# Normalised linear attention and a PReLU feed-forward on one core: batch 2 moves to tokens on partitions, with a refilled opening, a gated load and a spread of g by matmul

## The chip, the core and the metric

The kernel runs on one core of a Trainium2 chip. The metric is device time in microseconds (us). A core has a matrix engine (TensorE, PE in the profile), a vector engine (VectorE, DVE), an activation engine (ScalarE, ACT), a general-purpose engine (GpSimd, POOL) and a queue engine (SyncE, SP). Each takes its instructions in the order in which they were issued to it. Sixteen DMA engines move data between memory (HBM) and on-chip memory (SBUF); matmul results land in PSUM, of which this kernel uses eight buffers of 128 x 512 fp32.

## The reference

Eight batches of eight heads of 576 tokens with head dimension 64 pass a linear attention with an RMS norm per head; the heads are put side by side into 4608 tokens of width 512, which pass two matrix products with a PReLU between them.

```python
kv = np.einsum('bhsd,bhse->bhde', k, v)
out = np.einsum('bhsd,bhde->bhse', q, kv)
rms = np.sqrt(np.mean(out * out, axis=-1, keepdims=True) + 1e-06)
x = out / rms * g_norm            # then heads side by side: (4608, 512)
...
h = x @ w_in                      # 512 -> 2048
g = np.maximum(h, 0.0) + alpha * np.minimum(h, 0.0)
return g @ w_out                  # 2048 -> 512
```

## The kernel before, in words

All engines run in the order in which the program is written (`manual_schedule`), so the place of a call in the code is its place in each engine's queue.

**Tiles.** Tokens are cut into nine windows of 512. For each window w and each of 16 groups g of 128 hidden features, `m1_group` does four matmuls of 128 x 512 into a buffer `h_ps` (three of them, pool `psh`), ACT makes `m_sb` from it, DVE makes `gt` from both and so frees the buffer. `y_mm` then multiplies `gt` with `w_out`, 16 groups for each of four row blocks a, and `y_out` copies the sum on ACT and stores it with two DMAs from SP.

**The order of the feed-forward.** Block 0 runs the first stage of window 0 alone; the y phase (from line 512) runs row blocks 0 to 2 of its second stage; window 1's loop runs its first stage with row block 3 of window 0; from then on window w's first stage runs with window w-1's second stage, and the end is the second stage of the last window.

**Attention, feature form.** For the first `NB_PE` batches (3), features lie on partitions. For each of four pairs j of heads: `step_t` transposes q by five PE matmuls and a DVE copy; `step_kv` makes k'v of the pairs (five matmuls each) and masks it on DVE; `step_ot` makes the attention output and squares it on ACT; `ssq_mm` sums the squares by a matmul with a mask of ones, with ACT's Ln and Exp for the reciprocal root (`rstd`); `norm` multiplies on DVE into `xt`. The rows of these batches that reach past the last whole window are the tail (`step_tail_ot`, `step_tail_ssq`). `window_steps` lists these steps for windows 1 and 2, and the y phase and window 1's loop pop them one by one.

**Attention, token form.** For the other batches a DMA transpose from SP makes `qtm` from the regrouped q (`transpose_q`). A tile of 128 tokens is four matmuls of 128 columns and a square on ACT (`tile_a`), a DVE reduction (`tile_b`), Ln and Exp on ACT and a product `rg` with g on POOL (`tile_c`), and a DVE product `xrow` with DMA transposes from SP into `xm` (`tile_d`). `phase_steps` lays tile i's steps over three groups: a at the end of one, b and c in the next, d at the begin of the one after. c needs g in all partitions, `g_all`, which a DMA from SP brings in window 1.

**Loads.** `load_batch` issues six DMAs on POOL into one of two sets of staging buffers; `regroup` copies k and q into another order, on DVE or on POOL. A load waits in POOL's queue until an earlier one's semaphore is free (eight are in use), and so for DMAs eight places before it.

**Opening.** Batch 0 is loaded in halves of four heads. `keep_warm` runs matmuls whose results nobody reads.

Of the kernel before, what the change touches and what calls it, by code (L numbers as in the profile page):

```python
# [9 lines left out]
FP32 = mybir.dt.float32  # L10
FP16 = mybir.dt.float16
AF = mybir.ActivationFunctionType
ALU = mybir.AluOpType
# [4 lines left out]
def kernel(  # L18
# [11 lines left out]
    nc = tc.nc  # L30

    B, H, S, D = q.shape
# [3 lines left out]
    P = 128  # L36
    NPAIR = H // 2
    W = 512
    NW = N_TOK // W
# [6 lines left out]
    NC = D_MODEL // P  # L46
    assert NC == NPAIR and 0 < REM < P
    inv_d = 1.0 / D
    NB_PE = 3

    const_p = ctx.enter_context(tc.tile_pool(name="constp", bufs=1))
    w_p = ctx.enter_context(tc.tile_pool(name="weights", bufs=1))
# [52 lines left out]
    def regroup(b, nm, h0=0, h1=H, eng=None):  # L105
        (eng or nc.vector).tensor_copy(  # L106
            out=bufs[b % NBUF][nm][:, :, h0:h1, :].rearrange("p t h d -> p h t d"),
            in_=stages[b % NBUF][nm][:, h0:h1],
        )

    def load_batch(b):
        for nm in ("k", "q", "v"):
            load(b, nm)

    def regroup_batch(b):
        for nm in ("k", "q"):
            regroup(b, nm, eng=nc.gpsimd)

    for nm in "qkv":
# [12 lines left out]
    nc.vector.memset(mask32[64:128, 64:128], 1.0)  # L132
    mask16 = const_p.tile([P, P], FP16, name="mask16")
    nc.vector.tensor_copy(out=mask16[:], in_=mask32[:])
    warm16 = const_p.tile([P, W], FP16, name="warm16")
    nc.vector.memset(warm16[:], 0.5)
    eps_t = const_p.tile([P, 1], FP32, name="eps_t")
# [8 lines left out]
    nc.sync.dma_start(out=g2col[64:128, :], in_=g_norm[:].unsqueeze(1))  # L146
    alpha_row = const_p.tile([NF, P], FP32, name="alpha_row")
    nc.sync.dma_start(out=alpha_row[:], in_=moe_alpha[:].rearrange("(g p) -> g p", p=P))
    g_all = const_p.tile([P, D], FP32, name="g_all")


    WQ = 4
# [36 lines left out]
        load_w_out(i)  # L189


    def keep_warm(n):
        ps = ps_s.tile([P, W], FP32, name="warm_ps", tag="s")
        for i in range(n):
            nc.tensor.matmul(out=ps[:], lhsT=mask16[:], rhs=warm16[:], start=True, stop=True)

# [24 lines left out]
    def step_kv(b, j0=0, j1=NPAIR, pool=(ps_s, "s")):  # L221
        if j0 == 0:
            kv_sb = attn_p.tile([P, NPAIR, P], FP16, name="kv_sb")
            for j in range(NPAIR):
                kvs[b, j] = kv_sb[:, j, :]
            kvs[b] = kv_sb
        kv_ps = pool[0].tile([P, j1 - j0, P], FP32, name="kv_ps", tag=pool[1])
        for j in range(j0, j1):
            ks, vs = pair_cols(b, "k", j), pair_cols(b, "v", j)
            for t in range(NT):  # L230
                nc.tensor.matmul(  # L231
                    out=kv_ps[:, j - j0, :], lhsT=ks(t), rhs=vs(t),
                    start=(t == 0), stop=(t == NT - 1),
                )
        nc.vector.tensor_mul(  # L235
            out=kvs[b][:, j0:j1, :], in0=kv_ps[:],
            in1=mask32[:].unsqueeze(1).to_broadcast([P, j1 - j0, P]),
        )
# [8 lines left out]
    def step_ot(w, j, pool=None):  # L247
        if pool is not None:
            ot_ps = pool[0].tile([P, W], FP32, name="ot_ps", tag=pool[1])
        else:  # L250
            ot_ps = ps_o.tile([P, W], FP32, name="ot_ps", tag=f"o{j % 2}")
        n0 = w * W
        while n0 < (w + 1) * W:
            b = n0 // S
            n1 = min((b + 1) * S, (w + 1) * W)
            nc.tensor.matmul(  # L256
                out=ot_ps[:, n0 - w * W : n1 - w * W], lhsT=kvs[b, j],
                rhs=qts[b, j][:, n0 - b * S : n1 - b * S], start=True, stop=True,
            )
            n0 = n1  # L260
        sq = attn_p.tile([P, W], FP16, name="sq_sb")
        nc.scalar.activation(out=sq[:], in_=ot_ps[:], func=AF.Square)  # L262
        ots[w, j] = (ot_ps, sq)

    def step_ssq(w, j):
        ssq_mm(w, j)
        norm(w, j)

    def ssq_mm(w, j):
        ot_ps, sq = ots.pop((w, j))  # L270
        ssq_ps = ps_o.tile([P, W], FP32, name="ssq_ps", tag="o2")
        nc.tensor.matmul(out=ssq_ps[:], lhsT=mask16[:], rhs=sq[:], start=True, stop=True)  # L272
        rstd = attn_p.tile([P, W], FP32, name="rstd")
        nc.scalar.activation(  # L274
            out=rstd[:], in_=ssq_ps[:], func=AF.Ln, bias=eps_t[:], scale=inv_d,
        )
        nc.scalar.activation(out=rstd[:], in_=rstd[:], func=AF.Exp, bias=0.0, scale=-0.5)  # L277
        ots[w, j] = (ot_ps, rstd)

    def norm(w, j):  # L280
        ot_ps, rstd = ots.pop((w, j))
        xts[w, j] = xt_p.tile([P, W], FP16, name="xt", tag=f"xt{j}")
        nc.vector.scalar_tensor_tensor(  # L283
            out=xts[w, j][:], in0=ot_ps[:], scalar=g2col[:], in1=rstd[:],
            op0=ALU.mult, op1=ALU.mult,
        )
# [122 lines left out]
    def window_steps(w):  # L409

        order = "t0 kv t1 o0 t2 s0 o1 t3 s1 o2 - s2 o3 - s3".split()
        fn = {"t": step_t, "o": step_ot, "s": step_ssq}
        one = {"kv": lambda: step_kv(w), "-": lambda: None}
        return [one.get(x) or (lambda x=x: fn[x[0]](w, int(x[1]))) for x in order]
# [4 lines left out]
    def m1_mm(h_ps, w, g, cs):  # L419
        for c in cs:  # L420
            nc.tensor.matmul(  # L421
                out=h_ps[:], lhsT=w_in_blk(c, g), rhs=xt_of(w, c),
                start=(c == 0), stop=(c == NC - 1),
            )
# [11 lines left out]
    def m1_group(w, g):  # L436
        h_ps = ps_h.tile([P, W], FP32, name="h_ps", tag="h")
        m1_mm(h_ps, w, g, range(NC))
        m1_evac(h_ps, w, g)


    def y_mm(y, w, a, g):
        nc.tensor.matmul(  # L443
            out=y[:], lhsT=gts[w, g][:, a * P : (a + 1) * P], rhs=w_out_blk(g),
            start=(g == 0), stop=(g == NF - 1),
        )

    def y_out(y, w, a):
        y_sb = ysb_p.tile([P, D_MODEL], FP32, name="y_sb")
        nc.scalar.copy(out=y_sb[:], in_=y[:])  # L450
        for i in range(0, P, REM):
# [5 lines left out]
                rows = out[b * S + LONG : (b + 1) * S, :].rearrange("(p t) m -> t p m", t=TPP)  # L457
            nc.sync.dma_start(out=rows[t], in_=y_sb[i : i + REM, :])


    H_POOL = (ps_h, "h")
    keep_warm(10)
# [1 line left out]
    step_t(0, 0, H_POOL)  # L464
    step_t(0, 1, H_POOL)
    regroup(0, "k", 0, HH)
    keep_warm(3)
    step_kv(0, 0, 2)
    step_ot(0, 0)
    step_ot(0, 1)  # L470
    regroup(0, "q", HH, H)
# [11 lines left out]
    )  # L483
    regroup(0, "k", HH, H)
    ssq_mm(0, 0)
    ssq_mm(0, 1)
    step_kv(0, 2, 4)
    norm(0, 0)
    norm(0, 1)
    step_ot(0, 2)  # L490
    step_ot(0, 3, (ps_y, "y"))
    load_batch(2)
    first = [ps_h.tile([P, W], FP32, name="h_ps", tag="h") for g in range(3)]
    for g in range(3):
        m1_mm(first[g], 0, g, (0, 1))
    step_ssq(0, 2)
    keep_warm(2)
    step_ssq(0, 3)
    for g in range(3):
        m1_mm(first[g], 0, g, (2,))  # L500
    for g in range(3):
        m1_mm(first[g], 0, g, (3,))
        m1_evac(first[g], 0, g)
    for g in range(3, NF):
        m1_group(0, g)
        if g == 10:
            regroup(1, "k")
        if g == 14:
            regroup(1, "q")

# [9 lines left out]
    for g in range(NF):  # L520
        for a in range(AHEAD):
            y_mm(ys[a], 0, a, g)
            if a != 1 and steps and n - len(steps) < n * (AHEAD * g + a) // (AHEAD * (NF - 3)):
                steps.pop(0)()
    for a in range(AHEAD):
        y_out(ys[a], 0, a)
    regroup_batch(2)


    steps = window_steps(2)  # L530
    n = len(steps)
    y = ps_y.tile([P, W], FP32, name="y_ps", tag="y")
    for g in range(NF):
        if g == 3:
            load_batch(3)
            regroup_batch(3)
        m1_group(1, g)
        if g > 3 and steps:
            steps.pop(0)()
        y_mm(y, 0, AHEAD, g)  # L540
        if g > 3 and steps:
            steps.pop(0)()
        if g == NF - 4:
            nc.sync.dma_start(out=g_all[:], in_=g_norm[:].partition_broadcast(P))
        if g == NF - 3:
            transpose_q(3)
    y_out(y, 0, AHEAD)

    LOAD_G = 6
    for w in range(2, NW):
        steps = phase_steps(w + 1)
        for g in range(NF):
            if g == LOAD_G and w + 2 < B:
                load_batch(w + 2)
            a, part = divmod(g, TPW)
            if part == 0:
                pool, tag = ((ps_y, "y"), (ps_s, "s"))[a % 2]  # L560
                y = pool.tile([P, W], FP32, name="y_ps", tag=tag)
            begin, mid, end = steps.pop(0) if steps else ([], [], [])
            for f in begin:
                f()
            m1_group(w, g)
            for f in mid:
                f()
            for gg in range(part * TPW, (part + 1) * TPW):
                y_mm(y, w - 1, a, gg)
            if part == TPW - 1:  # L570
                y_out(y, w - 1, a)
            for f in end:
                f()
            if g == LOAD_G + 3 and w + 2 < B:
                regroup_batch(w + 2)
            if g == NF - 3 and w + 2 < B:
                transpose_q(w + 2)
# [35 lines left out]
```

## Time and profile before

| | |
|---|---|
| median of 6 runs (lowest to highest) | 304.49 us (303.85 to 305.35) |
| the profiled execution | 305.58 us |
| its span, first to last instruction | 303.8 us |
| mean granted clock | 0.989 |
| PE busy | 283.7 us, 93% of the span |
| DVE, ACT, POOL busy | 163.2, 156.5, 96.6 us |
| first-stage and second-stage matmuls of 128 x 512 | 1,152 |

The groups of instructions that weigh most, from the page (line, engine, operation, output<-inputs, shape and count, then busy us and mean ns of one, then the engine's idle time before them and what ended most of it):

```profile
L430 DVE SCALAR_TENSOR_TENSOR gt<-m_sb,beta_sb,h_ps 128x512 f16<-128x512 f32 x144 | 106.7, 744 | 79.3 <-ACT m_sb L428 78.2
L428 ACT ACTIVATE m_sb<-h_ps 128x512 f32<-128x512 f32 x144 | 85.7, 597 | 89.9 <-PE h_ps L421 89.7
L363 POOL TENSOR_TENSOR rg<-ss,g_all 128x512 f32<-128x512 f32 (+1 forms) x25 | 26.1, 1044 | 92.9 <-ACT ss L361 92.9
```

Matmuls are pipelined: the page gives a 128 x 512 one 379 ns from begin to end, while in a dense stretch one starts every 0.216 us (four in 0.86 us). An engine's busy share is an average over stages that have different limits; idle time of an engine that isn't the last to finish costs nothing.

### The profile page before, as it was taken

The page shows a single profiled execution, that of the slowest core. Times are in us where ns is not written, and L with a number is a line of the kernel's source. Part 1 is how long each engine was busy: PE and PEld are TensorE (multiplying, and loading weights), DVE is VectorE, ACT ScalarE, POOL GpSimd, SP SyncE. Part 2 cuts the span into 40 slices and gives each one's busy share as a digit, 9 for nine tenths or more (in the row PEclk, how much of TensorE's full clock was granted, in tenths as well). Part 3 has the DMA queues.
Part 4 walks back from the last instruction along what each step waited for, and adds up shares of the span by engine and source line. Part 5 has one row for each costly group of instructions (what it writes and reads, how often), then busy time and mean ns, then how long its engine had stood idle before and what let it go on. Part 6 is the DMA issues. An engine that isn't in the chain of part 4 may idle for free.

```text
span 303.8 us, 4204 instructions
## 1 busy us (share of the span) xinstructions
PE 283.7 (93%) x1526; PEld 136.5 (45%) x1526; DVE 163.2 (54%) x249; ACT 156.5 (52%) x298; POOL 96.6 (32%) x105
## 2 busy tenths in 40 slices
PE   5476999988999899999999999999999999999993
PEld 2232454453554355445544544455445444444441
DVE  4526953557665548544864585459546844344200
ACT  1256627749586348444843573458437544443320
POOL 9733315640018604660575055504101300000000
PEclk9969999999999999999999999999999999999999
DMA  7999999894117972995289839954311411112233
GB/s 88 171 206 200 203 204 184 124 216 90 35 35 99 197 181 28 144 224 127 54 118 212 155 68 146 185 122 74 75 35 37 95 35 35 37 39 55 46 70 69
DMA packets 61156, 34.33 MB, mean 113 GB/s; under 512 B 27840, under 2 KB 56528, under 8 KB 61136
## 3 DMA queue, kind: packets, MB, share of 16 engines
q0 software_dynamic: 29664, 18.35, 43.3%
q1 hardware_dynamic: 31472, 15.71, 24.1%
q8 instruction: 12, 0.20, 0.3%
q14 instruction: 8, 0.07, 0.1%
HBM read 36.74 MB, written 9.44 MB: 152 GB/s over the span
## 4 chain that ended last, share of the span: by engine, by line
PE 82%; ACT 5%; POOL 4%; DVE 3%; issue 2%; DMA 2%; POOLq 0%; ACTq 0%; DVEq 0%
PE h_ps L421 37%; PE y_ps L443 35%; PE kv_ps L231 3%; DMA qst<-in_q_dram 2%; PE otm_ps L339 2%; ACT rstd L274 2%; ACT m_sb L428 2%; POOL rg L363 1%; DVE gt L430 1%; PE qt_ps L210 1%; PE ssq_ps L272 1%; PE yc L443 1%; PE yb L443 1%; PE ya L443 1%; ACT rstd L277 1%
## 5 line engine op out<-in xcount | busy, mean ns | idle before, releaser
L430 DVE SCALAR_TENSOR_TENSOR gt<-m_sb,beta_sb,h_ps 128x512 f16<-128x512 f32 x144 | 106.7, 744 | 79.3 <-ACT m_sb L428 78.2
L443 PE MATMUL y_ps<-w_out_sb,gt 128*128 128x512 f16 x528 | 134.8, 379 | 0.0
L428 ACT ACTIVATE m_sb<-h_ps 128x512 f32<-128x512 f32 x144 | 85.7, 597 | 89.9 <-PE h_ps L421 89.7
L421 PE MATMUL h_ps<-xm,w_in_sb 128*128 128x512 f16 x384 | 98.5, 379 | 0.0
L421 PEld LDWEIGHTS <-w_in_sb 128*128 128x128 f16 x576 | 55.5, 98 | 67.4 <-issue 8.2
L443 PEld LDWEIGHTS <-gt 128*128 128x128 f16 x576 | 55.9, 98 | 65.9 <-issue 2.2
L363 POOL TENSOR_TENSOR rg<-ss,g_all 128x512 f32<-128x512 f32 (+1 forms) x25 | 26.1, 1044 | 92.9 <-ACT ss L361 92.9
L421 PE MATMUL h_ps<-xt,w_in_sb 128*128 128x512 f16 x192 | 48.4, 384 | 3.7 <-DVE gt L430 2.2
L450 ACT COPY y_sb<-y_ps 128x512 f32<-128x512 f32 x33 | 19.2, 582 | 17.5 <-PE y_ps L443 17.4
L351 DVE TENSOR_REDUCE ss<-sqm_sb 128x8 f32<-128x512 f32 (+1 forms) x25 | 17.1, 683 | 8.2 <-ACT sqm_sb L345 8.2
L106 POOL COPY ksb<-kst 128x2560 f16<-128x2560 f16 x6 | 13.9, 2318 | 21.6 <-DMA kst<-in_k_dram 21.6
L372 DVE TENSOR_TENSOR xrow<-otm_ps,rg 128x512 f16<-128x512 f32 (+1 forms) x25 | 17.0, 682 | 6.3 <-POOL rg L363 6.3
L345 ACT ACTIVATE sqm_sb<-otm_ps 128x512 f32<-128x512 f32 (+1 forms) x25 | 14.8, 593 | 6.9 <-PE otm_ps L339 6.9
L106 POOL COPY qsb<-qst 128x2560 f16<-128x2560 f16 x6 | 13.9, 2321 | 10.6 <-DMA qst<-in_q_dram 6.1
L283 DVE SCALAR_TENSOR_TENSOR xt<-ot_ps,g2col,rstd 128x512 f16<-128x512 f32 x12 | 8.9, 749 | 13.1 <-ACT rstd L277 13.1
L262 ACT ACTIVATE sq_sb<-ot_ps 128x512 f16<-128x512 f32 x12 | 6.9, 588 | 16.4 <-PE ot_ps L256 16.4
L231 PE MATMUL kv_ps<-vst,ksb 128*128 128x128 f16 x160 | 10.9, 225 | 2.8 <-DMA vst<-in_v_dram 1.4
L231 PEld LDWEIGHTS <-ksb 128*128 128x128 f16 x160 | 10.1, 101 | 6.5 <-issue 3.7
L274 ACT ACTIVATE rstd<-ssq_ps,eps_t 128x512 f32<-128x512 f32 x12 | 8.2, 685 | 6.5 <-PE ssq_ps L272 6.5
L339 PEld LDWEIGHTS <-qtm 128*128 128x128 f16 x100 | 7.7, 98 | 5.9
L339 PE MATMUL otm_ps<-kv_sb,qtm 128*128 128x128 f16 x100 | 9.7, 219 | 0.0
L235 DVE TENSOR_TENSOR kv_sb<-kv_ps,mask 128x512 f16<-128x512 f32 (+1 forms) x9 | 5.6, 627 | 6.3 <-PE kv_ps L231 6.3
(56 smaller groups left out, 134.7 us busy)
## 6 DMA issues: line engine op xcount, KB each, us to landing
out_dram<-y_sb SPq DMA_DIRECT2D x72, 128.0 KB, 2.4
kst<-in_k_dram POOLq DMA_DIRECT2D x7, 320.0 KB, 5.0
qst<-in_q_dram POOLq DMA_DIRECT2D x7, 320.0 KB, 8.5
vst<-in_v_dram POOLq DMA_DIRECT2D x7, 320.0 KB, 10.9
w_in_sb<-in_moe_w_in_dram POOLq DMA_DIRECT2D x4, 512.0 KB, 10.6
w_out_sb<-in_moe_w_out_dram POOLq DMA_DIRECT2D x4, 512.0 KB, 16.2
kst<-in_k_dram POOLq DMA_DIRECT2D x7, 256.0 KB, 6.5
qst<-in_q_dram POOLq DMA_DIRECT2D x7, 256.0 KB, 9.8
```

What stands on the lines that cost most here:

```text
L106: (eng or nc.vector).tensor_copy(out=bufs[b % NBUF][nm][:, :, h0:h1, :].rearrange("p t h d -> p h t d"), in_=stages[b % NBUF][nm][:, h0:h1],)
L231: nc.tensor.matmul(out=kv_ps[:, j - j0, :], lhsT=ks(t), rhs=vs(t), start=(t == 0), stop=(t == NT - 1),)
L339: nc.tensor.matmul(out=ot_ps[:, 2 * j : 2 * j + 2, :], lhsT=qtms[b][:, t * NPAIR + j, :], rhs=kvs[b, j], start=True, stop=True,)
L345: nc.scalar.activation(out=sq[0:n], in_=ot_ps[0:n], func=AF.Square)
L351: nc.vector.tensor_reduce(out=ss[0:n], in_=sq[0:n], op=ALU.add, axis=mybir.AxisListType.X,)
L363: nc.gpsimd.tensor_tensor(out=rg[0:n], in0=ss[0:n].unsqueeze(2).to_broadcast([n, H, D]), in1=g_all[0:n].unsqueeze(1).to_broadcast([n, H, D ...
L372: nc.vector.tensor_mul(out=x[0:n], in0=ot_ps[0:n], in1=rg[0:n])
L421: nc.tensor.matmul(out=h_ps[:], lhsT=w_in_blk(c, g), rhs=xt_of(w, c), start=(c == 0), stop=(c == NC - 1),)
L428: nc.scalar.activation(out=m_sb[:], in_=h_ps[:], func=AF.Relu, scale=-1.0)
L430: nc.vector.scalar_tensor_tensor(out=gt[:], in0=m_sb[:], scalar=beta_sb[:, g : g + 1], in1=h_ps[:], op0=ALU.mult, op1=ALU.add,)
L443: nc.tensor.matmul(out=y[:], lhsT=gts[w, g][:, a * P : (a + 1) * P], rhs=w_out_blk(g), start=(g == 0), stop=(g == NF - 1),)
L450: nc.scalar.copy(out=y_sb[:], in_=y[:])
```

## The change

- `NB_PE` goes from 3 to 2: batch 2 is computed in token form. The loop of window 2's attention steps within window 1 goes, and window 1 uses the general loop with `phase_steps`, keeping one y matmul for each group. The tail is then 128 columns wide and one step for all four pairs.
- The tiles of batch 2 come in windows 1 and 2. Its q is regrouped on DVE and transposed by DMA after group 9 of the y phase; its k is regrouped on DVE after group 13.
- The load of batch 3 stands after group 13 of the y phase. Ahead of it, a POOL copy of one element of batch 2's `qtm` waits for that transpose.
- From batch 2 on q is loaded and regrouped ahead of k.
- `g_all` is made after group 12 of block 0: DVE scales the identity by g, a matmul with ones spreads it over all partitions, DVE copies it out. The DMA for it goes.
- Opening: more `keep_warm` matmuls, before the first `step_ot`, between the sums of squares, and around the first groups; `norm` of pair 0 ahead of `step_kv` of pairs 2 and 3; the sum of squares of pair 2 after one group's first two matmuls, in a PSUM buffer of its own, where it came after three groups' and shared one.

```diff
-    NB_PE = 3
+    NB_PE = 2
...
     def load_batch(b):
-        for nm in ("k", "q", "v"):
+        for nm in ("q", "k", "v"):
             load(b, nm)
...
+    def spread_g():
+
+        diag = const_p.tile([P, D], FP32, name="diag")
+        nc.vector.tensor_scalar(
+            out=diag[0:D], in0=ident[0:D, 0:D], scalar1=g2col[0:D], scalar2=None, op0=ALU.mult,
+        )
+        g_ps = ps_y.tile([P, D], FP32, name="g_ps", tag="y")
+        nc.tensor.matmul(
+            out=g_ps[:], lhsT=ones32[0:D], rhs=diag[0:D], start=True, stop=True,
+        )
+        nc.vector.tensor_copy(out=g_all[:], in_=g_ps[:])
...
-    keep_warm(3)
+    keep_warm(4)
     step_kv(0, 0, 2)
+    keep_warm(2)
     step_ot(0, 0)
...
     ssq_mm(0, 0)
+    keep_warm(3)
     ssq_mm(0, 1)
+    norm(0, 0)
+    keep_warm(3)
     step_kv(0, 2, 4)
-    norm(0, 0)
     norm(0, 1)
-    step_ot(0, 2)
+    step_ot(0, 2, (ps_o, "o2"))
     step_ot(0, 3, (ps_y, "y"))
...
-    for g in range(3):
+    m1_mm(first[0], 0, 0, (0, 1))
+    ssq_mm(0, 2, (ps_s, "s"))
+    for g in (1, 2):
         m1_mm(first[g], 0, g, (0, 1))
-    step_ssq(0, 2)
-    keep_warm(2)
-    step_ssq(0, 3)
+    ssq_mm(0, 3, (ps_o, "o0"))
+    keep_warm(6, (ps_o, "o1"))
+    norm(0, 2)
+    norm(0, 3)
     for g in range(3):
         m1_mm(first[g], 0, g, (2,))
+    keep_warm(2, (ps_o, "o1"))
...
         if g == 10:
             regroup(1, "k")
+        if g == 12:
+            spread_g()
...
+        if g == 9:
+            regroup(2, "q")
+            transpose_q(2)
+        if g == 13:
+
+            gate = const_p.tile([1, 1], FP16, name="gate")
+            nc.gpsimd.tensor_copy(out=gate[:], in_=qtms[2][0:1, 0, 0:1])
+            load_batch(3)
+            regroup(2, "k")
     for a in range(AHEAD):
         y_out(ys[a], 0, a)
-    regroup_batch(2)
...
-    steps = window_steps(2)
-    n = len(steps)
-    y = ps_y.tile([P, W], FP32, name="y_ps", tag="y")
-    for g in range(NF):
-        if g == 3:
-            load_batch(3)
-            regroup_batch(3)
-        m1_group(1, g)
-        if g > 3 and steps:
-            steps.pop(0)()
-        y_mm(y, 0, AHEAD, g)
-        if g > 3 and steps:
-            steps.pop(0)()
-        if g == NF - 4:
-            nc.sync.dma_start(out=g_all[:], in_=g_norm[:].partition_broadcast(P))
-        if g == NF - 3:
-            transpose_q(3)
-    y_out(y, 0, AHEAD)
...
-    for w in range(2, NW):
+    for w in range(1, NW):
         steps = phase_steps(w + 1)
         for g in range(NF):
-            if g == LOAD_G and w + 2 < B:
+            if g == LOAD_G and 3 < w + 2 < B:
                 load_batch(w + 2)
             a, part = divmod(g, TPW)
...
+            parts = range(part * TPW, (part + 1) * TPW)
+            if w == 1:
+                a, parts = AHEAD, [g]
```

## The prediction

> **What bounds the kernel now.** I read the chain of waits first, then busy time by stage, then the granted clock in 2 us stretches, then the timeline around each wait.
>
> ```profile
> PE 82%; ACT 5%; POOL 4%; DVE 3%; issue 2%; DMA 2%; POOLq 0%; ACTq 0%; DVEq 0%
> ```
>
> TensorE (PE) sets the end, so only PE work removed and PE idle time removed count. By stage (columns: us, then PE, weight loads, DVE, ACT, POOL busy, PE clock, DMA share, GB/s):
>
> ```profile
> 0.00:26.72 26.72, 15.64 (x77) 7.08 (x78) 11.42 (x30) 10.04 (x16) 16.87 (x30) 0.87 1.12 162
> 26.72:38.37 11.65, 11.38 (x52) 5.07 (x52) 9.98 (x15) 7.31 (x13) 4.22 (x7) 1.00 1.34 202
> 38.37:54.51 16.14, 15.28 (x102) 7.72 (x101) 6.84 (x12) 8.10 (x14) 6.84 (x6) 1.00 1.19 178
> 54.51:78.92 24.41, 22.09 (x134) 11.04 (x133) 16.32 (x25) 16.82 (x31) 7.82 (x7) 1.00 0.79 134
> 78.92:110.16 31.24, 30.39 (x168) 14.95 (x167) 17.44 (x27) 18.21 (x36) 11.86 (x11) 1.00 0.74 124
> 110.16:139.80 29.64, 29.64 (x166) 14.54 (x164) 17.40 (x26) 15.82 (x32) 12.87 (x12) 1.00 0.82 133
> 139.80:169.66 29.86, 29.86 (x169) 14.74 (x168) 18.54 (x28) 16.83 (x35) 13.91 (x13) 1.00 0.75 128
> ```
>
> The rows are: opening; rest of block 0; y phase of window 0; window 1; windows 2, 3 and 4. From window 3 on PE never idles, and nothing there changes. All that can move is the first 110 us: 11 us idle in the opening, a window 1 of 24.4 us and a window 2 that takes 1.4 us more than window 4.
>
> The clock, in 2 us stretches (same columns):
>
> ```profile
> 12.00:14.00 2.00, 1.00 (x12) 0.83 (x13) 1.08 (x3) 0.71 (x2) 2.00 (x3) 0.96 1.33 176
> 14.00:16.00 2.00, 1.22 (x6) 0.52 (x5) 1.09 (x3) 1.49 (x3) 1.85 (x4) 0.50 1.27 205
> 18.00:20.00 2.00, 1.97 (x5) 0.71 (x5) 0.64 (x1) 1.09 (x2) 0.77 (x1) 0.50 1.24 205
> 20.00:22.00 2.00, 1.84 (x7) 0.69 (x6) 0.00 (x0) 0.55 (x1) 0.69 (x1) 0.84 1.24 206
> 50.00:52.00 2.00, 2.00 (x12) 0.82 (x11) 0.52 (x1) 1.50 (x4) 1.36 (x2) 1.00 1.40 198
> 52.00:54.00 2.00, 1.81 (x9) 0.78 (x8) 0.75 (x1) 1.50 (x4) 2.00 (x2) 1.00 0.47 69
> ```
>
> The clock is halved from about 13.8 to 20.7 us, when a 512-column matmul takes 0.43 instead of 0.216 us. The DMA engines are loaded to 52.8 us without a break: the loads through batch 2, in the order issued, set what can arrive when. The waits concerned, from the timeline (start, length, engine, line, in brackets the idle time before):
>
> ```profile
> 24.87 0.81 PE L421 MATMUL h_ps<-xt,w_in_sb 128*128 128x512 f16 x3 [0.43 <-DVE xt L283]
> ...
> 35.12 0.82 DVE L106 COPY ksb<-kst 128x2560 f16<-128x2560 f16 x1
> 35.85 2.06 DVE L430 SCALAR_TENSOR_TENSOR gt<-m_sb,beta_sb,h_ps 128x512 f16<-128x512 f32 x3
> ...
> 48.39 2.32 POOL L106 COPY ksb<-kst 128x2560 f16<-128x2560 f16 x1 [7.23 <-DMA kst<-in_k_dram]
> ...
> 61.69 1.28 PE L231 MATMUL kv_ps<-vst,ksb 128*128 128x128 f16 x20 [1.34 <-DVE qt_sb L219]
> ...
> 68.78 2.60 SPq L329 DMA_TRANSPOSE qtm<-qsb  x1
> ...
> 98.24 0.69 DVE L372 TENSOR_TENSOR xrow<-otm_ps,rg 128x512 f16<-128x512 f32 x1 [3.71 <-POOL rg L363]
> ...
> 99.64 1.02 PE L421 MATMUL h_ps<-xt,w_in_sb 128*128 128x512 f16 x4 [0.85 <-DVE gt L430]
> ```
>
> **What the Trainium skill says.** "TensorE: Matmul & The Clock Gate", Part 1 (What's actually happening): the array's clock is halved or full, decided over free-running stretches of 3.4 us, and drops after an idle one. The trace agrees on length (13.8 to 20.7 is two of them) but not on "idle": in the 3.4 us before the drop PE was busy 1.7 us, while 2.0 us busy (20.7 to 24.1) kept the clock. The same page (Architectural detail) says VectorE and ScalarE queues are strictly first in, first out; the trace agrees (at 98.24 DVE stands 3.71 us behind one operand, and the evacuations after it stand too). "DMA: Bandwidth & Descriptors", Issuing engines are not separate DMA queues: transfers from SP and POOL share the same 16 engines. Here a transpose of q lands in 4.1 to 5.7 us, those of x in 2.3 to 7.8.
>
> **Part 1, the opening.** Before, the chain to the third stage of block 0 is: kv of pairs 2, 3, ot, six first-stage matmuls at half clock, ssq, two ACT operations (0.69+0.63), the same again, norm (0.75), and the last quarter of the first groups at 24.87. After, fillers cover 11.2-11.6, 14.0-14.7 and 15.2-15.9; ssq of pair 2 comes after two first-stage matmuls, not six, and has its own buffer. At full clock: kv 15.9-16.6, mask on DVE to 17.0 (norm of pair 0 is already done), ot 17.1-17.6, squares to 18.6; w_in's first quarter lands at 18.1 (POOL's queue waits for it then), so two matmuls 18.1-18.5, ssq 18.55-18.9, Ln and Exp of pair 2 to 20.3, of pair 3 to 21.6, norm to 22.4, last quarter at 22.45. Gain 2.4. If the clock stays halved over 13.8-17.2, the fillers take 2.6 us instead of 1.3 and the same sum ends at 23.4: gain 1.5. The 0.43 us filler before ot lifts PE's busy time before 13.8 from 1.7 to 2.1 us, above the 2.0 that kept the clock, so I take 2.4. The filler delays ot by 0.43, which the wait for q's second half (12.4) hides.
>
> **Part 2, g spread in block 0.** The DMA of g (0.65 on SP) goes, which nothing waited for. In its place, after group 12, a DVE operation, an fp32 matmul and a DVE copy. The matmul waits for `diag`, which stands in DVE's queue behind the evacuation of group 12, and PE does nothing else meanwhile. Group 12's matmuls end at 35.36; DVE, 0.8 us late from the copy of k (35.12), evacuates it 36.54-37.22; diag, at the 0.17 of the smallest tensor-scalar here, to 37.4; the matmul 0.2 to 0.5 (alpha's fp32 one takes 0.23), so group 13 starts 2.3 us later. In return two of PE's waits for freed buffers there (0.27 before an h, 0.17 before yc) go. Following DVE on (copy of g, groups 13 and 14, q of batch 1, 0.82), the first transpose of the y phase moves from 39.9 to 41.9: cost 2.0, bounds 1.6 and 2.3. It cannot be free, for no PE work is ordered between.
>
> **Part 3, y phase.** q of batch 2 is now loaded where k was, so it lands at 48.4. Its regroup moves from POOL (2.32) to DVE (0.82), behind the second norm: about 50.5-51.3. SP issues the transpose 51.35-53.95, before the outputs at 54.9, so these aren't delayed; it lands 4.2 later, 55.5. Loads end at 52.8, so the two barely meet. k's regroup stands behind the last norm (55.1): 55.1-55.9, and kv of batch 2 waits for it: 0.5 us of PE, counted in part 4. The gate stands on POOL until 55.5; behind it are six issues of batch 3's load (4.2 us, to 59.8 instead of 57.7) and the first rg (needed at 63). The load ends some 2 us later, near 70; its k regroup ends by 73, before window 2 wants it at 78. Cost 0; 1:1 for PE where that slack is used up.
>
> **Part 4, window 1.** Removed: 20 transposes, 4 ot and 4 ssq (1.1 and 8 x 0.216); added: three tiles of 4 x 0.055 and the tail, 1,024 columns (0.43), which before came in window 2. PE: 80 x 0.216 = 17.3, kv 1.12, tail 0.43, tiles 0.66, kv's wait 0.5, last norm's 0.15: 20.2 against 24.4. But the groups are short here (5 matmuls, 1.08), and each tile brings ACT 0.60+0.30+0.21 and DVE 0.69+0.69. Placed by queue order with these durations, DVE frees h of groups 4, 5 and 6 at 65.85, 67.95 and 69.6, where PE comes at 64.95, 67.0 and 69.05: 2.4 us of waits. Window 1 ends at 77.15, not 78.92: gain 1.8. Bounds: no waits (gain 4.2), or all of the removed work given back (0).
>
> **Part 5, window 2.** Two tail steps and three tiles become five tiles, as in window 4. The tiles start at once, so their rg are through before the next load's six issues at group 6; the 3.71 us DVE wait at 98.24 and PE's 0.85 go. 31.24 becomes window 4's 29.86: gain 1.4; the tail work is in that. I take 1.2, for the first POOL copies may overlap an rg.
>
> Sum: -2.4 + 2.0 + 0 - 1.8 - 1.2 = -3.4. The profiled execution took 305.58 (span 303.8), so 302.2; against the median 304.49, which is 1.09 lower, **301.1**.
>
> **Rivals.**
> - *Window 1 is set by DVE and ACT.* DVE was 67% and ACT 69% busy there already, with shorter groups to come; against: the PE work removed is as sure. Gain of part 4 gone: 302.9.
> - *No waits there.* The buffers hold three groups, and back-to-back evacuations take 0.69, not 0.75. Part 4 gives 4.2: 298.7.
> - *The clock falls behind the spread.* Two us of PE idle in block 0 leave about 1.4 us busy in a 3.4 us stretch that contains them, and 1.7 dropped the clock at 13.8. Against: the wait may straddle two stretches. Price 6.9 us at half speed, 3.45: 304.5.
> - *Slower: the transpose of q of batch 2 is late.* PE reaches the first tile near 60 and stands in order until qtm lands; gate, load and rg stand with it. It has 4.5 us of slack beyond 4.2; PE pays 1:1 past 8.7 us. The x transposes took up to 7.8 instead of 2.5 among loads, three times; three times 4.2 lands at 64.3, costing 4.3: 305.4. It decides against the gain from 63.5 on. Against: loads end before it.
>
> **How the numbers follow.** Forecast 0.48 (its own range 300.2 to 302.2), window 1 bound 0.16, no waits 0.12, clock 0.12, late transpose 0.12. 0.3% (0.9 us) is about what a measurement here can tell from no change. Faster 0.73 (the first three, less 0.03 for costs at their worst), same 0.14, slower 0.13. The range 299.0 to 304.6 leaves out the late transpose and half of the no-waits case.
>
> **What would show it.** Right: clock 1.00 over 14 to 20 us; last quarter of the first groups near 22.5; PE idle about 2 us after group 12, released by DVE diag; window 1 about 22.7 us with waits for gt in groups 7 to 9; window 2 about 29.9 with no wait of xrow for rg beyond 1 us. Wrong: qtm landing after 60, kv of batch 2 waiting for a load, or a clock of 0.5 after 15 us.

## The result, and the profile after

| | before | after |
|---|---|---|
| median (lowest to highest) | 304.58 us (302.48 to 306.76), 35 runs | 302.23 us (301.27 to 303.28), 16 runs |
| profiled execution, span, mean clock | 305.58, 303.8, 0.989 | 302.95, 301.0, 0.994 |

Ratio 0.9925, 95% interval 0.9905 to 0.9946: 2.3 us faster, where 3.4 were forecast. The chain of waits of the kernel after has PE at 85% where it had 82%:

```profile
PE 85%; POOL 3%; ACT 3%; DVE 3%; DMA 3%; issue 2%; POOLq 0%; ACTq 0%
```

Busy time by stage of the kernel after (us, then PE, weight loads, DVE, ACT, POOL busy, PE clock, DMA share, GB/s), in the cuts of the table before: opening, rest of block 0, y phase, windows 1 and 2:

```profile
0.00:23.17 23.17, 16.64 (x92) 7.60 (x93) 11.51 (x31) 9.93 (x16) 16.60 (x29) 1.00 1.11 164
23.17:38.56 15.39, 13.44 (x54) 5.72 (x54) 10.75 (x17) 7.31 (x13) 6.30 (x8) 0.89 1.33 202
38.56:54.41 15.85, 15.16 (x102) 7.72 (x101) 7.28 (x13) 8.10 (x14) 0.68 (x1) 1.00 1.29 184
54.41:77.00 22.59, 19.95 (x118) 9.76 (x117) 16.86 (x25) 14.43 (x30) 11.93 (x12) 1.00 1.14 178
77.00:107.20 30.20, 30.20 (x171) 14.96 (x170) 19.19 (x29) 17.31 (x36) 13.92 (x13) 1.00 0.77 130
```

The opening is 3.55 us shorter and keeps the clock throughout; its end in PE's timeline:

```profile
17.04 0.61 PE L422 MATMUL h_ps<-xt,w_in_sb 128*128 128x512 f16 x2 [0.21 <-DMA w_in_sb<-in_moe_w_in_dram]
...
21.32 0.81 PE L422 MATMUL h_ps<-xt,w_in_sb 128*128 128x512 f16 x3
```

Block 0 then gives 3.74 back, at a clock of 0.89. Windows 1 and 2 bring the rest. The product k'v (kv) of batch 3 starts window 2's work and that of batch 4 window 3's, first in the kernel before, then in the kernel after:

```profile
79.78 1.28 PE L231 MATMUL kv_ps<-vst,ksb 128*128 128x128 f16 x20
...
110.86 1.28 PE L231 MATMUL kv_ps<-vst,ksb 128*128 128x128 f16 x20
```

```profile
78.06 1.28 PE L232 MATMUL kv_ps<-vst,ksb 128*128 128x128 f16 x20
...
107.92 1.28 PE L232 MATMUL kv_ps<-vst,ksb 128*128 128x128 f16 x20
```

The start of window 1 is only 0.10 earlier, so window 1 gained 1.6 us and window 2 gained 1.2.

The timeline of PE in block 0 of the kernel after (start, length, engine, line, in brackets the idle time before):

```profile
23.17 8.79 PE L422 MATMUL h_ps<-xt,w_in_sb 128*128 128x512 f16 x40 [1.03 <-DVE gt L431]
33.91 0.43 PE L470 MATMUL g_ps<-diag,ones 64*128 64x64 f32 x2 [1.95 <-DVE diag L466]
34.28 4.45 PE L422 MATMUL h_ps<-xt,w_in_sb 128*128 128x512 f16 x12
```

and the same kernel in stretches of 2 us (columns as above):

```profile
32.00:34.00 2.00, 0.09 (x1) 0.09 (x1) 1.86 (x4) 0.59 (x1) 0.66 (x2) 1.00 1.35 197
34.00:36.00 2.00, 2.00 (x7) 0.87 (x8) 0.22 (x1) 0.11 (x1) 1.28 (x2) 0.66 1.37 204
36.00:38.00 2.00, 2.00 (x6) 0.76 (x5) 0.75 (x1) 0.89 (x2) 0.75 (x2) 0.50 1.24 206
```

PE stands 1.95 us for `diag`, and behind that the clock is halved for some 3.4 us: the 12 matmuls of groups 13 to 15 take 4.28 us until the y phase instead of 2.6 at 0.216. This is the prediction's clock rival, and it comes on top of the forecast.

PE's waits from there on, in the timeline of the kernel after:

```profile
55.80 1.29 PE L232 MATMUL kv_ps<-vst,ksb 128*128 128x128 f16 x20 [0.36 <-DVE ksb L106]
...
61.11 0.38 PE L340 MATMUL otm_ps<-kv_sb,qtm 128*128 128x128 f16 x4 [1.20 <-DVE xm L314]
...
67.83 1.02 PE L422 MATMUL h_ps<-xt,w_in_sb 128*128 128x512 f16 x4 [0.49 <-DVE gt L431]
69.65 1.02 PE L422 MATMUL h_ps<-xt,w_in_sb 128*128 128x512 f16 x4 [0.58 <-DVE gt L431]
```

The second was in no sum of the forecast: the first tile takes the PSUM buffer o0, which the tail's `xm` still reads (`tag=f"o{i % 2}"`). In window 2 neither PE's wait of 0.85 nor the wait of `xrow` for `rg` of 3.71 is left; the longest of `xrow` is 0.50. The transpose of q and the gate, on SP's and POOL's queues:

```profile
51.18 3.53 SPq L330 DMA_TRANSPOSE qtm<-qsb  x1
...
56.53 0.18 POOL L555 COPY gate<-qtm 1x1 f16<-1x1 f16 x1 [16.54 <-DMA qtm<-qsb]
```

It landed at 56.5, 4.6 us ahead of the first tile and 3.4 ahead of PE's coming to that tile (59.9, where it stands 1.20 us for `xm`).

### The profile page after: what moved, and what is told of

Same layout as the page of the kernel before. It is cut to its first block, busy times and chain, and to the rows that moved or that the text cites. A ratio compares the mean times of both kernels' runs of the same rounds, so it can differ in the third digit from the quotient of the medians.

```text
span 301.0 us, 4238 instructions
## 1 busy us (share of the span) xinstructions
PE 284.4 (94%) x1530; PEld 136.4 (45%) x1530; DVE 166.8 (55%) x255; ACT 153.1 (51%) x298; POOL 98.5 (33%) x109
## 4 chain that ended last, share of the span: by engine, by line
PE 85%; POOL 3%; ACT 3%; DVE 3%; DMA 3%; issue 2%; POOLq 0%; ACTq 0%
PE h_ps L422 39%; PE y_ps L444 37%; PE kv_ps L232 3%; DMA w_in_sb<-in_moe_w_in_dram 3%; PE otm_ps L340 2%; DVE gt L431 1%; ACT m_sb L429 1%; PE yc L444 1%; PE yb L444 1%; PE ya L444 1%; PE warm_ps L196 1%; PE ssq_ps L273 1%; DVE ksb L106 1%; PE qt_ps L211 0%; POOL vst L100 0%
## 5 line engine op out<-in xcount | busy, mean ns | idle before, releaser
L422 PE MATMUL h_ps<-xm,w_in_sb 128*128 128x512 f16 x448 | 115.0, 379 | 0.0
L364 POOL TENSOR_TENSOR rg<-ss,g_all 128x512 f32<-128x512 f32 (+1 forms) x30 | 31.3, 1042 | 86.1 <-ACT ss L362 85.2
L422 PE MATMUL h_ps<-xt,w_in_sb 128*128 128x512 f16 x128 | 32.9, 395 | 2.3 <-DVE gt L431 2.1
L352 DVE TENSOR_REDUCE ss<-sqm_sb 128x8 f32<-128x512 f32 (+1 forms) x30 | 20.5, 683 | 9.6 <-ACT sqm_sb L346 9.6
L346 ACT ACTIVATE sqm_sb<-otm_ps 128x512 f32<-128x512 f32 (+1 forms) x30 | 17.8, 592 | 9.3 <-PE otm_ps L340 9.3
L373 DVE TENSOR_TENSOR xrow<-otm_ps,rg 128x512 f16<-128x512 f32 (+1 forms) x30 | 20.4, 681 | 3.6 <-POOL rg L364 3.6
L196 PE MATMUL warm_ps<-warm,mask 128*128 128x512 f16 x30 | 9.6, 457 | 3.8 <-DVE eps_t L140 3.3
L263 ACT ACTIVATE sq_sb<-ot_ps 128x512 f16<-128x512 f32 x8 | 4.5, 589 | 15.6 <-PE ot_ps L257 15.6
L232 PE MATMUL kv_ps<-vst,ksb 128*128 128x128 f16 x160 | 10.4, 219 | 1.2 <-DMA vst<-in_v_dram 0.8
L284 DVE SCALAR_TENSOR_TENSOR xt<-ot_ps,g2col,rstd 128x512 f16<-128x512 f32 x8 | 6.0, 749 | 9.1 <-ACT rstd L278 9.1
L359 ACT ACTIVATE ss<-ss,eps_t 128x8 f32<-128x8 f32 (+1 forms) x30 | 9.0, 301 | 3.1 <-DVE ss L352 3.1
## 6 DMA issues: line engine op xcount, KB each, us to landing
w_in_sb<-in_moe_w_in_dram POOLq DMA_DIRECT2D x4, 512.0 KB, 10.4
```

Of the source, the lines that this page charges most:

```text
L232: nc.tensor.matmul(out=kv_ps[:, j - j0, :], lhsT=ks(t), rhs=vs(t), start=(t == 0), stop=(t == NT - 1),)
L346: nc.scalar.activation(out=sq[0:n], in_=ot_ps[0:n], func=AF.Square)
L352: nc.vector.tensor_reduce(out=ss[0:n], in_=sq[0:n], op=ALU.add, axis=mybir.AxisListType.X,)
L364: nc.gpsimd.tensor_tensor(out=rg[0:n], in0=ss[0:n].unsqueeze(2).to_broadcast([n, H, D]), in1=g_all[0:n].unsqueeze(1).to_broadcast([n, H, D ...
L373: nc.vector.tensor_mul(out=x[0:n], in0=ot_ps[0:n], in1=rg[0:n])
L422: nc.tensor.matmul(out=h_ps[:], lhsT=w_in_blk(c, g), rhs=xt_of(w, c), start=(c == 0), stop=(c == NC - 1),)
```

## The clock behind the spread of the times

Every execution comes with a mean granted clock. 124 executions of the kernel before, which ran beside the experiments, fall into steps of about 0.005, which is one halved stretch of 3.4 us in 301 (half of 3.4, over 301, is 0.0056). Eight more, of 307.26 us and above, with clocks of 0.975 to 0.981, are left out:

| mean clock | executions of before | median us (lowest to highest) |
|---|---|---|
| 0.996 to 1.0 | 29 | 302.97 (302.56 to 303.65) |
| 0.992 to 0.995 | 44 | 304.33 (303.45 to 305.21) |
| 0.986 to 0.991 | 24 | 305.20 (304.19 to 306.43) |
| 0.980 to 0.985 | 27 | 306.58 (305.04 to 307.13) |

So the time follows the number of halved stretches over most of the spread of 302.5 to 307, and the profiled execution of before, at 0.989, had two. Of the 16 executions of after, ten had 0.996 or more (median 302.00) and six less (302.94): three at 0.993 or 0.994, which fits one halved stretch, and three at 0.990, which fits two. At a kept clock the whole change is worth about 1.0 us; the other 1.3 of the median would then be stretches that the opening no longer loses, less those that the spread of g loses. I give this number for the experiments too, as "at a kept clock": the median of the executions at 0.996 or more, and how many of them. It sorts executions by what came of them; that those which keep the clock differ in nothing else, the arrival of their loads for instance, isn't shown. They are few and from several chips (the kernel before at a kept clock has 302.77 to 303.16 by chip), so differences under 0.4 us between them mean little.

## The experiments

Each was timed against the kernel before on the same chip.

**The opening alone** (the kernel before, with the `keep_warm`, `ssq_mm` and `norm` lines of the change's opening and their buffers, nothing else; the middle of it):

```diff
-    for g in range(3):
+    m1_mm(first[0], 0, 0, (0, 1))
+    ssq_mm(0, 2, (ps_s, "s"))
+    for g in (1, 2):
         m1_mm(first[g], 0, g, (0, 1))
-    step_ssq(0, 2)
-    keep_warm(2)
-    step_ssq(0, 3)
+    ssq_mm(0, 3, (ps_o, "o0"))
+    keep_warm(6, (ps_o, "o1"))
+    norm(0, 2)
+    norm(0, 3)
```

> The kernel before with the changed opening alone (fillers, order of norms and sums, PSUM buffers), nothing else. Theory: clock 1.00 through the opening, last quarter of the first groups near 22.4 instead of 24.9 (2.4 us earlier), and all of it reaches the end: 302.1. Rival (part of the 3.5 us seen in the changed kernel's trace were faster loads of that execution, or the y phase waits for w_out's first quarter, which landed at 35.95): under 1.5 us gained, above 303.

Measured 302.44 us, ratio 0.9926 (0.9903 to 0.9948); at a kept clock 302.43 (21 of 22). It gives as much as the whole change, 2.3 us by the ratio. But where the kernel before keeps its clock too, it is worth only 0.5 us against 302.97 (0.7 against 303.16, the nine on the same chip); the rest of the 2.3 goes with its nearly always keeping it.

**Nine of the opening's fillers alone**, to part clock and order:

```diff
-    keep_warm(3)
+    keep_warm(4)
     step_kv(0, 0, 2)
+    keep_warm(2)
...
     ssq_mm(0, 0)
+    keep_warm(3)
     ssq_mm(0, 1)
+    keep_warm(3)
```

> The kernel before with nothing of the change but nine of the opening's fillers (one more before kv of pairs 0 and 1, two before the first ot, three after each of the sums of squares of pairs 0 and 1); order and buffers of the opening as before. Of 98 executions of the kernel before, the 20 with a mean clock of 0.996 or more have a median of 303.0 us, the 78 with less lie from 303.45 up. Theory (the opening's gain is mostly the clock it keeps, the shorter order of its sums of squares is worth about 0.5 us): nearly all executions have a mean clock of 0.995 or more, median 302.7 to 303.3 us, between the opening of the change alone (302.44) and the kernel before (304.2 to 305.0). Rival 1 (the gain is the order of the sums of squares and their buffers): about 304.5 us, as before. Rival 2 (order and clock both, with the full gain only together): about 303.7 us, the clock dropping once in many executions.

Measured 303.49 us (302.84 to 304.61), ratio 0.9976 (0.9954 to 0.9997). Of 22 executions 18 had 0.996 or more (median 303.38). The fillers mostly keep the clock, where 29 of 124 executions of the kernel before did, but 303.49 lies 0.2 above the theory's band. At a kept clock these fillers cost about 0.4 us themselves (302.97 to 303.38), and the rest of the opening is worth 0.9 (303.38 to 302.43), not 0.5. By the ratios the nine fillers bring 0.7 of the opening's 2.3 us, so that the second rival is right that the gain needs more than them, though not in its clock. The rest is the order, the PSUM buffers and the eight fillers around the first groups (for two before); no run parts these. Its stretches of 2 us (columns as above):

```profile
14.00:16.00 2.00, 1.32 (x13) 0.83 (x12) 0.58 (x2) 1.40 (x3) 1.01 (x2) 1.00 1.24 206
16.00:18.00 2.00, 1.45 (x7) 0.67 (x7) 1.16 (x2) 1.03 (x2) 0.77 (x1) 1.00 1.24 207
20.00:22.00 2.00, 0.81 (x3) 0.29 (x3) 1.43 (x2) 1.26 (x3) 0.19 (x1) 1.00 1.25 207
22.00:24.00 2.00, 0.84 (x4) 0.32 (x4) 0.90 (x3) 1.46 (x3) 0.49 (x1) 1.00 1.26 203
```

PE is busy 1.65 us of the four from 20 to 24 and the clock stays at 1.00, while in the kernel before 1.7 of 3.4 us came ahead of a drop: how much busy time in which stretch keeps the clock isn't settled here.

**g by DMA in the opening instead of the spread**, which was to price the spread:

```diff
+    g_all = const_p.tile([P, D], FP32, name="g_all")
+    nc.sync.dma_start(out=g_all[:], in_=g_norm[:].partition_broadcast(P))
...
-        if g == 12:
-            spread_g()
```

> The changed kernel, but g comes into all partitions by one DMA in the opening; the spread after group 12 of block 0 is gone. Theory (PE's wait for diag costs 2.0 us, and in some executions it also drops the clock for 3.4 us, another 1.7): stretch from group 3 of block 0 to the y phase falls from 15.4 to about 11.7 us, no clock below 1 after 7 us, time 2 to 3.7 us under the changed kernel, so 298.5 to 300.2. Rival (the wait only fills a gap that the loads or DVE's backlog would open anyway): the same time as the changed kernel, 302.2, within 0.5.

Measured 302.90 us, ratio 0.9945 (0.9923 to 0.9966): no gain over the kernel after. PE no longer waits in block 0, but DVE's timeline shows a loss earlier, first here, then in the kernel after:

```profile
9.56 0.49 DVE L106 COPY qsb<-qst 128x1280 f16<-128x1280 f16 x1 [5.13 <-DMA qst<-in_q_dram]
```

```profile
5.59 0.64 DVE L106 COPY qsb<-qst 128x1280 f16<-128x1280 f16 x1 [1.17 <-DMA qst<-in_q_dram]
```

The DMA of g, 32 KB to 128 partitions, was issued at 2.64 and landed 6.6 us later; the first load of q beside it came 4 us late, and in the stretch from 14 to 16 us the clock is 0.50. This execution, of 304.10 us, is one of the slowest of the 22, so the 4 us are not typical; but 13 of the 22 have a mean clock under 0.996, where the opening alone had one of 22. The run prices an early DMA of g, not the spread.

**Batch 2 alone, with g by DMA** (the last kernel with the opening of the kernel before; of its edit):

```diff
-    keep_warm(4)
+    keep_warm(3)
     step_kv(0, 0, 2)
-    keep_warm(2)
...
-    m1_mm(first[0], 0, 0, (0, 1))
-    ssq_mm(0, 2, (ps_s, "s"))
-    for g in (1, 2):
+    for g in range(3):
         m1_mm(first[g], 0, g, (0, 1))
```

> The changed kernel with the opening of before, and g by a DMA in the opening: the move of batch 2 alone. Theory: window 1 falls from 24.4 to 22.8 us and window 2 from 31.2 to 30.0: 3.0 us, 301.5. Rival (the gain of windows 1 and 2 hangs on the earlier opening): under 1 us.

Measured 305.40 us, ratio 1.0025 (0.9995 to 1.0055). The early DMA of g stands in the way again: 11 of its 14 executions had a mean clock of 0.985 or less, where the same kernel with the early spread in place of the DMA, below, has 3 of 22. By which path is not shown: in its trace the first copy of q is at 6.96, hardly later than in the profiled executions without such a DMA (5.57 to 6.73). It doesn't tell what batch 2 is worth.

**The wait for `diag` filled** (eight fillers ahead of the matmul in `spread_g`).

```diff
+        keep_warm(8)
         g_ps = ps_y.tile([P, D], FP32, name="g_ps", tag="y")
```

> The changed kernel with eight unread matmuls (1.7 us) ahead of the spread's matmul. The wait stays, but PE is busy during it. Theory that the clock drop is a cost of its own: clock stays 1.00, y phase 1.5 to 1.7 us earlier than in the changed kernel's profiled execution, median lower by up to 1 us (the drop came in part of the executions only), about 301.3. Rival (the drop doesn't come from the wait, or costs nothing because DVE is behind anyway): no change, 302.2.

Measured 301.78 us, ratio 0.9926 (0.9901 to 0.9952), every one of 6 executions at 0.996 or more. PE's timeline:

```profile
23.52 8.79 PE L422 MATMUL h_ps<-xt,w_in_sb 128*128 128x512 f16 x40 [1.03 <-DVE gt L431]
34.27 0.43 PE L471 MATMUL g_ps<-diag,ones 64*128 64x64 f32 x2 [0.22 <-DVE diag L466]
...
37.23 0.38 PE L444 MATMUL ya<-w_out_sb,gt 128*128 128x512 f16 x1
```

From the first row to the y phase it is 13.71 us. Before it was 11.65: the spread at this place costs 2.06, and the other 1.68 of the kernel after's 3.74 were the clock. What that brings in time isn't shown: the medians differ by 0.45, but the ratios to the kernel before (0.9926 and 0.9925) don't. For the clock there are more executions: in six kernels with the changed opening in which PE doesn't stand idle for `diag` in block 0 and g comes by no DMA (this one, and those from the early spread on that keep the opening and the gate), 49 of 52 have 0.996 or more, in the kernel after ten of 16.

**The spread early**, where the opening waits for its loads anyway (`spread_g()` moved).

```diff
     keep_warm(4)
+    spread_g()
     step_kv(0, 0, 2)
...
-        if g == 12:
-            spread_g()
```

> The changed kernel with the spread of g moved into the opening, behind the first k regroup and ahead of the first kv, where PE waits for v anyway; same three instructions, no DMA. Theory (the wait behind group 12 is the price that eats the opening's gain): no PE wait for diag in block 0, clock 1.00 there, y phase begins near 36.5 instead of 38.6, time 2 us or more under the changed kernel: 299.5 to 300.3. Rival (the loads are the real limit: w_out's first quarter, v of batch 1 and v of batch 2 can't come earlier): what is gained in block 0 is lost as waits for loads in the y phase or at kv of batch 2; within 0.7 of 302.2.

Measured 301.07 us (300.56 to 301.39), ratio 0.9888 (0.9834 to 0.9942), between the theory's number and the rival's; both hold in part. Block 0 is back at 11.65 us (24.02 to 35.67), so the spread costs PE nothing there, and the y phase starts 2.9 us earlier than in the kernel after. Only 1.6 of them are left 20 us on, in PE's timeline:

```profile
54.23 1.28 PE L232 MATMUL kv_ps<-vst,ksb 128*128 128x128 f16 x20 [1.38 <-DMA vst<-in_v_dram]
```

The loads are the next limit: v of batch 2 isn't there yet (in the run with the tiles apart, below, PE stands 1.81 us for it).

**Batch 2 alone, with the early spread** (the last kernel, by the same edit to the opening of the kernel before).

> The opening of before with batch 2 in token form, the gate, the loads as in the change, and the spread of g in the idle stretch of the opening, so without the DMA that stood among the first loads. Theory: windows 1 and 2 give 3.0 us by themselves: about 301.6. Rival (batch 2's move gives nothing unless the opening is early): 304 or more.

Measured 301.90 us, ratio 0.9920 (0.9894 to 0.9945); at a kept clock 301.15 (6 of 22). Its kv of batch 2 starts at 55.04 without waiting for v:

```profile
55.04 1.29 PE L232 MATMUL kv_ps<-vst,ksb 128*128 128x128 f16 x20 [0.36 <-DVE ksb L106]
```

So at a kept clock batch 2's move is worth 1.8 us (302.97 to 301.15), and the opening on top of it next to nothing (301.07, the run before): what the opening brings forward runs into the loads, as far as the two traces show it. In the median it still adds 0.8, which goes with the clock (16 of the 22 here are under 0.996, none of the six there).

**No gate** (on the kernel after):

```diff
-            gate = const_p.tile([1, 1], FP16, name="gate")
-            nc.gpsimd.tensor_copy(out=gate[:], in_=qtms[2][0:1, 0, 0:1])
             load_batch(3)
```

> The changed kernel without the POOL copy that waits for the transpose of q of batch 2. The load of batch 3 then starts near 40 us, right behind v of batch 2. Theory of the late transpose: qtm, which landed about 5.3 us after its issue with the gate, lands several us later among the loads; beyond about 61 us PE waits for it at the first tile: slower than the changed kernel by 1 to 5 us, with the x transposes late too. Rival (the transpose has enough slack, and an earlier load helps): within 0.5 of 302.2.

Measured 309.78 us, ratio 1.0181 (1.0125 to 1.0237). SP's queue, and PE's timeline at the first tile:

```profile
51.78 7.61 SPq L330 DMA_TRANSPOSE qtm<-qsb  x1
59.44 3.81 SPq L459 DMA_DIRECT2D out_dram<-y_sb  x6
```

```profile
67.06 0.61 PE L340 MATMUL otm_ps<-kv_sb,qtm 128*128 128x128 f16 x4 [6.55 <-DMA qtm<-qsb]
```

Among the loads of batch 3 the transpose of q lands 15 us after its issue instead of 5.3, and even SP's own issue of it takes 7.61 instead of 3.53. The prediction's slower rival is a real mechanism; the gate is what keeps it out, and is worth 7.5 us: 6.55 of waiting, and the clock behind it (0.50 from 66 to 72 us in the trace; all six executions have a mean clock of 0.987 or less).

**The tail in buffers of its own, and the tiles two groups apart** (on the early spread).

```diff
-        ot_ps = ps_o.tile([P, JT, TAIL], FP32, name="ot_ps", tag=f"o{i % 2}")
+        ot_ps = ps_o.tile([P, JT, TAIL], FP32, name="ot_ps", tag="o2")
...
-        ssq_ps = ps_o.tile([P, JT, TAIL], FP32, name="ssq_ps", tag="o2")
+        ssq_ps = ps_s.tile([P, JT, TAIL], FP32, name="ssq_ps", tag="s")
...
+        if w == NB_PE:
+            todo = [x for t in todo for x in (t, None)][:-1]
...
```

> The kernel with the early spread, and in window 1 the tail in PSUM buffers that no tile uses next, and the three tiles of batch 2 begun two groups apart instead of one. Theory (window 1's PE waits are one of 1.2 us for the tail's buffer and about 1.1 for h buffers that a crowded DVE frees late): both go, window 1 falls from 22.8 to about 20.6 us; time about 2 us under the early spread, near 298. Rival (x transposes or other loads end window 1): within 0.7 of the early spread.

Measured 302.04 us, ratio 0.9915 (0.9891 to 0.9938): worse than the early spread by 1 us, on the same chip. The wait for `xm` went, but PE's waits for `gt` grew from 1.07 to 2.9:

```profile
63.10 1.02 PE L424 MATMUL h_ps<-xt,w_in_sb 128*128 128x512 f16 x4 [0.54 <-DVE gt L433]
66.77 1.02 PE L424 MATMUL h_ps<-xt,w_in_sb 128*128 128x512 f16 x4 [1.18 <-DVE gt L433]
70.44 1.02 PE L424 MATMUL h_ps<-xt,w_in_sb 128*128 128x512 f16 x4 [1.18 <-DVE gt L433]
```

DVE's timeline of the same run says why:

```profile
61.70 0.69 DVE L373 TENSOR_TENSOR xrow<-otm_ps,rg 128x512 f16<-128x512 f32 x1 [1.08 <-POOL rg L364]
...
65.37 0.69 DVE L373 TENSOR_TENSOR xrow<-otm_ps,rg 128x512 f16<-128x512 f32 x1 [1.07 <-POOL rg L364]
```

`xrow` stands in order ahead of the next `gt` and waits for POOL's `rg` each time, 3.2 us in all from 58 to 76 us, where the early spread alone has 0.5: with tiles one group apart, the next tile's work fills that time.

**The tail's buffers alone; kv of batch 2 one group later; both** (on the early spread, the tiles one group apart again). The buffers are those of the diff above, without what it does to `todo`; for kv:

```diff
-            steps[0][1].append(lambda: step_kv(w))
+            steps[1 if w == NB_PE else 0][1].append(lambda: step_kv(w))
```

> The change with the early spread of g, and the tail's two products in buffers of their own (ot_ps in o2, ssq_ps in the buffer s), the tiles one group apart as in the change. Theory (the 1.20 us at the first tile is the wait for o0, which the tail's xm reads last): the wait goes and nothing takes its place, about 299.9 us beside 301.07. Rival (the tiles are what VectorE and the tail queue on; starting them 1.2 us sooner only brings their waits for gt sooner): the wait at the first tile goes and the waits of h_ps for gt grow from 1.07 to about 2.2 us, about 301 us.

> The change with the early spread of g, and kv of batch 2 issued in the second group of window 1 instead of in the first. Theory (once the opening and block 0 are short, the loads set when kv of batch 2 can run, and TensorE stands 1.38 us for v of batch 2; a group later v is there, and the 1.1 us of kv lie where TensorE stood 1.20 us for the tail's xm): both waits go, 1.4 + 1.1 = 2.5 us less than with the early spread alone, so about 298.6 us beside 301.07. Rival 1 (the same time comes back as waits of h_ps for gt in the tiles, which then follow the tail more closely): the two waits go, the waits for gt grow from 1.07 to 2.5 us or more, about 300 to 301 us. Rival 2 (the load of v isn't just 1.4 us late, it moves on behind the transposes): kv still waits, a group later, about 301 us.

> Both of the others: kv of batch 2 a group later and the tail in buffers of its own. If kv alone already fills the wait at the first tile, this gives what kv a group later gives, about 298.6 us, within 0.3 us. If the waits for gt take the place of whatever is removed, about 300 to 301 us, like the others.

| | us | ratio (interval) | window 1 starts | kv of batch 3 starts |
|---|---|---|---|---|
| early spread | 301.07 | 0.9888 (0.9834 to 0.9942) | 51.81 | 76.48 |
| tail's buffers | 300.43 | 0.9874 (0.9837 to 0.9910) | 50.87 | 75.31 |
| kv later | 300.24 | 0.9868 (0.9827 to 0.9909) | 51.29 | 75.24 |
| both | 300.30 | 0.9866 (0.9829 to 0.9902) | 51.11 | 75.28 |

All end at the same place. From the start of window 1 to kv of batch 3 they save 0.2, 0.7 and 0.5 us; the rest of the 1.2 in the last column arose ahead of window 1, where the profiled execution of the early spread got its first q late (copied at 6.73, in the other three at 5.58 to 5.93). The tail's buffers take away the wait for `xm`, kv later takes away that for v, and both together leave 0.5 of the latter. PE's waits between 50 and 80 us (us in total, times, longest), of the kernel with kv later and of that with the tail's buffers:

```profile
PE h_ps L422 <- DVE gt L431: 1.7, 3, 0.6
PE otm_ps L340 <- DVE xm L314: 1.2, 1, 1.2
```

```profile
PE h_ps L422 <- DVE gt L431: 1.7, 3, 0.6
PE kv_ps L232 <- DVE gt L431: 1.7, 1, 1.7
```

In both the waits of `h_ps` for `gt` grew from 1.07 to 1.7, and with the tail's buffers alone kv still waits 1.7. With kv later the wait for `xm` stayed too, because the step list puts kv ahead of the tail's sum of squares and not behind it, as the theory had it. The best of the three, 300.24, can't be told from the others, and hardly from the early spread (the intervals overlap); all four lie below the change's 302.23.

## Why the prediction was right, and where its sizes were off

The forecast of 301.1 was 1.1 us under the median. The direction and the mechanisms held: each part that it named shows in the trace, with the sizes below. That the total came so near is partly luck, since the opening's surplus (1.15) and the lost clock stretch (1.68) pull against each other. Of its signs of being wrong one appeared, a clock of 0.5 after 15 us, behind the spread.

- *Part 1, the opening: -2.4 forecast, -3.55 in the trace.* The clock stayed at 1.00, and the last quarter of the first groups came at 21.32 instead of 22.45. About 1.05 us of that came from a load: the first quarter of w_in landed at 17.0, not 18.1, in this execution. That 2.0 us of busy time keep the clock was not put to the test, for PE was busy 2.87 us from 10.4 to 13.8, not 2.1. The step that was mis-sized is how the gain carries over to the median: the sum was made against an execution that had two halved stretches and then lowered by a constant 1.09. Where before keeps its clock the opening is worth 0.5.
- *Part 2, the spread: +2.0 forecast, +3.74 in the trace.* The term itself was right (2.06 with the wait filled). The other 1.68 are the clock, which the prediction had as a rival at 0.12 and priced at two stretches, 3.45; it was one, in the profiled execution. Five more of the 16 have a mean clock that fits one or two; where they lost it is not on record.
- *Part 3, the y phase: 0 forecast, -0.3.* The gate opened at 56.5 (forecast 55.5), with 3.4 us to spare before PE came to the tile, not 4.5; the slower rival came about when the gate was taken away.
- *Part 4, window 1: -1.8 forecast, -1.6.* Right in sum, from other terms. Waits for `gt` came in two groups, 1.07 us in all, not 2.4 in three; the 1.20 us for the tail's buffer was not foreseen; kv waited 0.36 for k's copy (0.5 forecast).
- *Part 5, window 2: -1.2 forecast, -1.2*, by the step given.

The sum of the trace, 303.8 to 301.0, is -2.8; the parts that the prediction added (-3.4) fell short by the clock behind the spread, less the opening's surplus of 1.15; the rest of the terms moved by 0.3 or less. What the sum did not ask is whether the parts add up. By their ratios the opening and batch 2 alone bring 2.3 and 2.4 us, and together, with the early spread, 3.4; the interval of the last, 1.8 to 5.1 us, doesn't rule out the full 4.7, so that the evidence that they don't is the wait for v in the trace.

## What to carry to other kernels

Before summing gains from one profiled execution, look at the mean clock of all executions: here one kernel spread over 4 us by how many 3.4 us stretches it lost, and what an edit that keeps the clock brings depends on what the median execution loses, not on what the profiled one lost. An operation that PE must wait for belongs where PE is waiting for loads anyway, and a stall in a dense stretch costs its own length plus, at times, a halved stretch behind it. Two gains that lie on both sides of a load may not add up: ask when the load lands once the first is made.

## What the runs showed of the hardware

- The clock of 0.5 came behind 1.95 us of PE waiting in a dense stretch; ten of 16 executions of the same code have a mean clock that leaves no room for it, and with the wait filled all six. The Trainium skill, "TensorE: Matmul & The Clock Gate", Part 1 (What's actually happening), says that the stretches over which activity is judged run free of the kernel's start; that it comes in some executions only fits this, but no run here shows where a stretch begins.
- A DMA transpose among loads from POOL slowed from 5.3 to 15 us, and its issue on SP from 3.53 to 7.61.
- A 32 KB broadcast to 128 partitions beside the first loads took 6.6 us in the one trace and 4.4 in the other. In the two kernels that have it, 13 of 22 and 13 of 14 executions have a mean clock under 0.996, where the same openings without it have one of 22 (the opening alone) and 16 of 22 (batch 2 alone, with the early spread).
